# Putting the additions on x in program order between the operand work of h

## The chip, the cores and the metric

One Trainium2 chip, one of its cores. The metric is the device time of one execution in microseconds (us). The kernel before takes 975.35 us, the median of three runs from 972.98 to 976.16.

## The reference, cut to what matters

Attention over keys and values that are averaged in groups of eight, and behind it a gated feed-forward layer, all in fp32:

```python
k_p = k.reshape(B, H, Sp, 8, D).mean(axis=3)        # B = H = 8, S = 576, Sp = 72, D = 64
v_p = v.reshape(B, H, Sp, 8, D).mean(axis=3)
scores = scale * np.matmul(q, k_p.transpose(0, 1, 3, 2))
attn = softmax(scores)
x = np.matmul(attn, v_p)                            # as 4608 tokens x 512
gate = 1.0 / (1.0 + np.exp(-(x @ w_gate)))          # w_gate, w_val: 512 x 1536
return (gate * (x @ w_val) @ w_out)                 # w_out: 1536 x 512
```

## The kernel before, in words

The 4608 tokens are 12 blocks of 384. Blocks 0 and 1 are worked through by a written-out list in a first pass of about 230 us, which also splits the weights into parts and stores them in device memory. The other ten blocks go in five passes, n = 1 to 5, two blocks each. A pass has two stages on TensorE:

- **The gate and value stage** (`hidden`, its matmuls are L621). x of two blocks times the two weight matrices, as two-by-two block products in the seven-product form (Winograd's): products m = 1 to 7 need x11, x12, x21, x22 and sums of them. Every fp32 operand is split into a high and a low part (`fp32r`), so each product term is three matmuls, and one product is six. The results leave PSUM through ScalarE (ACT) copies (L627), VectorE (DVE) additions into a tile `y` (L633), the sigmoid on ACT (L639) and a DVE multiplication (L642), which gives h.
- **The output stage** (`second_sums`, L834). h times w_out in the same seven-product form: 21 units of 12 matmuls, three for each of m = 1, 5, 6, 2, 3, 7, 4. I call them unit 0 to unit 20. The operand of a unit is made by `operand`: DVE sums where needed (`minus`, L766), an ACT cast for the high part (L797) and a DVE subtraction for the low part (L798), into one of four buffers. It is traced two units ahead. After units 11, 14, 17 and 20 the results go out: by DVE (L812), and the last by ACT (L810), into a tile named `o` that shares the two buffers of `y`, and from there by a DMA (L814).

Beside this, the attention of the next two blocks runs, in small steps between the products: scores (L454), exponential (L508, which needs another ACT table than the sigmoid, so an `ACT_TABLE_LOAD` before it and one before the next sigmoid), a transposition of the residual columns (L523) and of the main columns (L542) on TensorE, the product with v (L463) and a copy into `xs` (L553).

x's own operands for the next pass are made by `operands`, a generator of seven steps. Each step is an addition on DVE where one is needed (`combine`, L590), an ACT cast (L167) and a DVE subtraction (L168), the latter two in `split`. The steps come in the order m = 1, 5, 6, 2, 3, 7, 4. One step is drawn after each of units 8, 10, 12, 14, 16, 18 and 20 (`next(build, None)`, L852). The last pass has no next one, so there are four output stages that do this, n = 1 to 4.

What sets the order of instructions on an engine in the five passes: a scheduler, which goes by its own estimate of when each operand is ready and puts an instruction that it thinks ready ahead of others. It may move an instruction far from the place where it was traced. `tc.keep_in_program_order` adds an edge, without a semaphore, from the instruction that was traced just before on the same engine. `in_turn` does that when `tied[0]` is set; L590, L167 and L168 pass through it. Before, the flag is set only for some weight sums of pass 1. All DMAs are issued by SyncE (SP), in its own order, on one queue.

Of the kernel before, what the change touches and what calls it, by code (L numbers as in the profile page):

```python
# [124 lines left out]
def attention_then_ffn(ctx: ExitStack, tc: tile.TileContext, qT, kT, vm, vr, vn, sums8, wgv, wo, const, out, outT):  # L125
# [33 lines left out]
    tied = [False]  # L159
# [198 lines left out]
    def reload_s(m, q):  # L358

        t = opool.tile([P, 2, 2, HALF], F32R, name="oparts")  # L360
        if m < 4:
            half = slice(HALF, DM) if m == 3 else slice(0, HALF)
            for k in range(2):
                f = 4 * q + 2 * k + (m > 1)
                nc.sync.dma_start(t[:, k].bitcast(F32), kept_o[f][:, :, half].bitcast(F32))
        else:
            nc.sync.dma_start(t.rearrange("p k h n -> p k (h n)").bitcast(F32), kept_s[m, q].bitcast(F32))
        oparts[m, q] = t
# [243 lines left out]
    def product(kind, p, m, stays=False):  # L612

        b = {1: "A", 6: "A", 7: "A", 4: "A", 2: "B", 5: "C", 3: "C"}[m]
        if m in (1, 2, 5):
            bank[kind, b] = ps.tile([P, BT], F32, name="chain", tag=CHAIN["GV".index(kind) * 3 + "ABC".index(b)])
        t, w, x = bank[kind, b], parts[kind, p, m] if stays else parts.pop((kind, p, m)), xo[m]
        for c in range(NC // 2):
            a = slice(c * P, (c + 1) * P)
            for k, (h, y) in enumerate(((0, 0), (0, 1), (1, 0))):  # L620
                nc.tensor.matmul(  # L621
                    t, lhsT=w[:, h, a], rhs=x[:, y, c],
                    start=(m in (1, 2, 5) and c == 0 and k == 0), stop=(c == 1 and k == 2), skip_group_check=True,
                )
        if m in (1, 5, 6):
            s = snap.tile([P, BT], F32, name=f"s{kind}{m}")
            nc.scalar.copy(s, t)  # L627
            seen[kind, m] = s
            return
        q = {2: (0, 0), 3: (0, 1), 7: (1, 1), 4: (1, 0)}[m]  # L630
        if m != 4:
            y = two.tile([P, BT], F32, name="y", tag="y")
            nc.vector.tensor_tensor(out=y, in0=t, in1=seen[kind, {2: 1, 3: 6, 7: 5}[m]], op=ALU.add)  # L633
        else:
            y = t
        if kind == "G":
            if m in (2, 7):
                gates[q[0]] = snap.tile([P, 2, BT], F32, name=f"gate{q[0]}")
            nc.scalar.activation(gates[q[0]][:, q[1]], y, AF.Sigmoid)  # L639
        else:  # L640
            f = 2 * p + q[1]
            nc.vector.tensor_tensor(  # L642
                out=hb[f // 4][:, f % 4, q[0] * BT:(q[0] + 1) * BT], in0=y, in1=gates[q[0]][:, q[1]], op=ALU.mult
            )
# [123 lines left out]
    def first_sums(q):  # L768

        at = len(s1)  # L770
        if at == 0:
            s1[None] = big.tile([P, 2, 2, BT], F32, name="s1", tag="big")
            at = 1
        s1[q] = s1[None][:, at - 1] if at < 3 else snap.tile([P, 2, BT], F32, name="s1", tag="gate0")
        minus(s1[q], quarter(q, 1, 0), quarter(q, 1, 1), ALU.add)
        if at < 3:
            third_sums(q)
# [9 lines left out]
    def operand(m, q, n):  # L787

        if m == 6:
            minus(s1[q], s1[q], quarter(q, 0, 0))  # L790
        if m == 3:
            minus(s1[q], quarter(q, 0, 1), s1[q])
        if m == 7 and q == qs[n][2]:
            third_sums(q)
        x = s1[q] if m in (5, 6, 3) else quarter(q, *{1: (0, 0), 2: (0, 1), 7: (1, 0), 4: (1, 1)}[m])
        hs = big.tile([P, 2, 2, BT], F32R, name="hs", tag="big")
        nc.scalar.copy(hs[:, 0], x)  # L797
        nc.vector.tensor_tensor(out=hs[:, 1], in0=x, in1=hs[:, 0].bitcast(F32), op=ALU.subtract)  # L798
        halves[m, q] = hs
# [3 lines left out]
    def second_sums(n, last, build, later):  # L803
        A, B_, C = ("b4", "b5"), ("b0", "b3"), ("b1", "b2")
        acc, seen2 = {}, {}

        def result(side, half, c, bank, add):
            t = two.tile([P, BT], F32, name="o", tag="y")
            if add is None:
                nc.scalar.copy(t, bank)  # L810
            else:
                nc.vector.tensor_tensor(out=t, in0=bank, in1=add, op=ALU.add)  # L812
            r, a = (half * 2 + c) * P, (2 * n - 2 + side) * BT
            nc.sync.dma_start(outT[r:r + P, a:a + BT], t)  # L814

        units = [(m, q) for m in (1, 5, 6, 2, 3, 7, 4) for q in qs[n]]
        for u in units[:2]:
            reload_s(*u)
        for i, (m, q) in enumerate(units):
            if i + 2 < len(units):  # L820
                reload_s(*units[i + 2])
            if i == 1:
                first_sums(qs[n][2])
            if i + 2 < len(units):
                operand(*units[i + 2], n)
            hs = halves.pop((m, q))
            w = oparts.pop((m, q))
            name = {1: "A", 6: "A", 7: "A", 4: "A", 2: "B", 5: "C", 3: "C"}[m]
            for k in range(2):
                for c in range(2):  # L830
                    if i % 3 == 0 and k == 0 and m in (1, 2, 5):
                        acc[name, c] = ps.tile([P, BT], F32, name="acc", tag={"A": A, "B": B_, "C": C}[name][c])
                    for t, (h, y) in enumerate(((0, 0), (0, 1), (1, 0))):
                        nc.tensor.matmul(  # L834
                            acc[name, c], lhsT=w[:, k, h, c * P:(c + 1) * P], rhs=hs[:, y, k],
                            start=(m in (1, 2, 5) and i % 3 == 0 and k == 0 and t == 0), stop=(i % 3 == 2 and k == 1 and t == 2),
                            skip_group_check=True,
                        )
                if i == 0 and k == 1:
                    product("V", TURNS[n][-1], 4, not last)  # L840
            if i % 3 == 2:
                for c in range(2):
                    t = acc[name, c]
                    if m in (1, 5, 6):
                        s = snap.tile([P, BT], F32, name=f"s{'GV'[c]}{m}")
                        nc.scalar.copy(s, t)
                        seen2[m, c] = s
                    else:
                        side, half = {2: (0, 0), 3: (0, 1), 7: (1, 1), 4: (1, 0)}[m]
                        result(side, half, c, t, None if m == 4 else seen2[{2: 1, 3: 6, 7: 5}[m], c])  # L850
            if i >= 8 and i % 2 == 0:
                next(build, None)  # L852
        for _ in build:
            pass
        for _ in range(3):
            next(later, None)
        s1.clear()
# [329 lines left out]
    for n in range(NB // 2):  # L1187
        last = 2 * n + 2 == NB
        tasks, later = ahead[n:n + 2]
        steady[0] = n > 1  # L1190
        if n == 0:
            continue
        if n == 1:
            hidden_second(tasks)
        else:
            hidden(last, tasks, n)
        if last:
            build = iter(())
        else:
            build = operands()  # L1200
        if n < 1:
            second(tasks, build)
        else:
            second_sums(n, last, build, later)
# [46 lines left out]
```

## Time and profile before

| | |
|---|---|
| median of three runs | 975.35 us (972.98, 975.35, 976.16) |
| the profiled execution | 973.47 us, its span 971.7 us |
| granted TensorE clock | 0.993 |
| busy: TensorE matmul, weight loads, DVE, ACT | 97%, 93%, 73%, 57% |
| output stages, by the trace | about 326 to 381, 483 to 536, 632 to 689, 786 to 838 and 922 to 972 us |

Rows are named by engine and line. PE is the matmul side of TensorE and PEld its weight loads, DVE is VectorE, ACT is ScalarE, and SPq is the queue of SyncE that issues the DMAs. A name such as `hs<-s,hs` says what is written and what is read. In the profile's lists of waits the three numbers are the sum in us, how often, and the longest. In its timeline a row begins with the start and the duration in us, and brackets give the idle time of the engine just before and what ended it. Matmuls overlap: one of 384 columns lasts some 0.34 us in a row, but the next one starts 0.175 us after it.

### The profile page before, as it was taken

To read this page: it belongs to the slowest core of one execution; us is meant where nothing else is said; L and a number is where in the kernel's file an instruction comes from. 1 tells how busy PE (TensorE), PEld (TensorE's weight loads), DVE (VectorE), ACT (ScalarE), POOL (GpSimd) and SP (SyncE) were. 2 spreads that over 40 slices of the span, in tenths; PEclk is the share of its full clock that TensorE was granted. 3 is DMA by queue.
4 is the path that set the end of the run, shared out by engine and by line. 5 is a ranking of instruction groups with operands and counts; after the bars stand their busy time and mean duration, and the time that the engine had idled before them with its cause. 6 is when DMAs were issued, how large, how long until landed. Compare 5 with 4: busy or idle time off the path is not lost.

```text
span 971.7 us, 15360 instructions
## 1 busy us (share of the span) xinstructions
PE 939.0 (97%) x5400; PEld 907.2 (93%) x5400; DVE 706.8 (73%) x1231; ACT 557.5 (57%) x1142; POOL 47.5 (5%) x67
## 2 busy tenths in 40 slices
PE   5899999999998999999999999999999999999998
PEld 4689998889998999999999999989999999999998
DVE  7999998787888878767796566599366578244474
ACT  6898966554666656645664555556355555233342
POOL 1210000000000000000000000000000000000000
PEclk8899999999999999999999999999999999999999
DMA  9978987769877377997479878567876637877566
GB/s 317 343 264 311 315 305 219 257 229 352 296 269 245 131 241 247 351 362 247 129 230 277 264 239 275 177 184 255 271 257 221 211 120 227 283 247 251 163 205 228
DMA packets 109883, 243.22 MB, mean 250 GB/s; under 512 B 11376, under 2 KB 45936, under 8 KB 108272
## 3 DMA queue, kind: packets, MB, share of 16 engines
q1 hardware_dynamic: 109808, 242.26, 75.1%
q8 instruction: 43, 0.70, 0.3%
q14 instruction: 32, 0.26, 0.1%
HBM read 191.88 MB, written 50.33 MB: 249 GB/s over the span
## 4 chain that ended last, share of the span: by engine, by line
PE 71%; DVE 15%; DMA 7%; ACT 4%; issue 2%; SPq 0%; DVEq 0%; ACTq 0%
PE chain L621 38%; PE acc L834 18%; PE chain L661 5%; PE acc L1147 3%; PE sc L454 3%; PE av L463 2%; DVE s L766 2%; DVE hs L798 1%; DMA out<-o 1%; DMA raw<-in_wgv 1%; DVE raw L197 1%; DVE w L199 1%; PE tp L542 1%; DVE zs L975 1%; DMA parts<-keptG1A 1%
## 5 line engine op out<-in xcount | busy, mean ns | idle before, releaser
L621 PE MATMUL chain<-xo,parts 128*128 128x384 f32 x2436 | 457.5, 341 | 7.6 <-ACT sG L627 2.5
L621 PEld LDWEIGHTS chain<-xo,parts 128*128 128x128 f32 x2436 | 424.0, 188 | 12.1 <-ACT sG L627 3.7
L834 PE MATMUL acc<-hs,oparts 128*128 128x384 f32 x1260 | 229.2, 336 | 3.2 <-DVE hs L798 2.8
L834 PEld LDWEIGHTS acc<-hs,oparts 128*128 128x128 f32 x1260 | 218.2, 188 | 6.0 <-DVE hs L798 4.4
L633 DVE TENSOR_TENSOR y<-chain,sG 128x384 f32<-128x384 f32 x87 | 47.8, 552 | 79.1 <-ACT sG L627 27.6
L661 PE MATMUL chain<-xo,parts 128*128 128x384 f32 x504 | 93.7, 340 | 0.8 <-ACT xs L1086 0.8
L661 PEld LDWEIGHTS chain<-xo,parts 128*128 128x128 f32 x504 | 87.9, 188 | 2.6 <-ACT xs L1086 1.1
L627 ACT COPY sG<-chain 128x384 f32<-128x384 f32 x87 | 41.5, 477 | 55.5 <-PE chain L621 55.1
L633 DVE TENSOR_TENSOR y<-chain,sV 128x384 f32<-128x384 f32 x87 | 47.5, 550 | 35.1 <-PE chain L621 26.4
L798 DVE TENSOR_TENSOR hs<-h,hs 128x768 fp32r<-128x768 f32 x60 | 58.1, 973 | 17.1 <-ACT hs L797 17.1
L627 ACT COPY sV<-chain 128x384 f32<-128x384 f32 x87 | 41.3, 476 | 50.0 <-PE chain L621 45.5
L639 ACT ACTIVATE gate<-y 128x384 f32<-128x384 f32 x87 | 45.5, 525 | 41.2 <-DVE y L633 40.7
L797 ACT CAST hs<-h 128x768 fp32r<-128x768 f32 x60 | 49.9, 834 | 25.4 <-PE acc L834 25.1
L536 POOL TENSOR_TENSOR pm<-e,rz 128x384 f32<-128x384 f32 x32 | 29.2, 912 | 610.7 <-DVE rz L516 224.7
L797 ACT CAST hs<-s 128x768 fp32r<-128x768 f32 x45 | 37.0, 835 | 34.4 <-PE acc L834 22.7
L1147 PE MATMUL acc<-oparts,hs 128*128 128x512 f32 x216 | 51.7, 392 | 0.4 <-DVE hs L1137 0.4
L642 DVE TENSOR_TENSOR h<-y,gate 128x384 f32<-128x384 f32 x87 | 49.0, 567 | 1.8
L798 DVE TENSOR_TENSOR hs<-s,hs 128x768 fp32r<-128x768 f32 x45 | 42.5, 954 | 8.3 <-ACT hs L797 8.0
L1147 PEld LDWEIGHTS acc<-oparts,hs 128*128 128x128 f32 x216 | 40.2, 188 | 8.7 <-DVE hs L1137 0.8
L454 PE MATMUL sc<-kbd,raw 128*128 128x144 f32 (+1 forms) x280 | 47.6, 308 | 0.0
L454 PEld LDWEIGHTS sc<-kbd,raw 128*128 128x128 f32 (+1 forms) x280 | 38.3, 187 | 6.6 <-issue 4.0
L546 DVE TENSOR_TENSOR pl<-tp,ph 128x384 fp32r<-128x384 f32 x32 | 17.6, 551 | 26.7 <-ACT ph L545 26.7
(186 smaller groups left out, 1182.0 us busy)
## 6 DMA issues: line engine op xcount, KB each, us to landing
oparts<-keptS SPq DMA_DIRECT2D x60, 512.0 KB, 4.4
oparts<-keptO SPq DMA_DIRECT2D x90, 256.0 KB, 3.8
raw<-in_wgv SPq DMA_DIRECT2D x12, 1024.0 KB, 6.7
raw<-in_qT SPq DMA_DIRECT2D x42, 192.0 KB, 4.3
out<-o SPq DMA_DIRECT2D x40, 192.0 KB, 4.3
raw<-in_kT SPq DMA_DIRECT2D x26, 288.0 KB, 4.1
raw<-in_vm SPq DMA_DIRECT2D x28, 256.0 KB, 4.1
raw_o<-in_wo SPq DMA_DIRECT2D x12, 512.0 KB, 4.4
```

The costliest lines, as they stand in the source:

```text
L454: nc.tensor.matmul(sc[lo - i * P:hi - i * P, i], lhsT=q[:, lo:hi], rhs=kbd[slot(b, p)], start=True, stop=True)
L536: nc.gpsimd.tensor_tensor(out=pm, in0=e[:, n, :, :KM], in1=rz[:, n, :, None].broadcast_to([P, 2 * QT, KM]), op=ALU.mult)
L621: nc.tensor.matmul(t, lhsT=w[:, h, a], rhs=x[:, y, c], start=(m in (1, 2, 5) and c == 0 and k == 0), stop=(c == 1 and k == 2), skip_group_ ...
L627: nc.scalar.copy(s, t)
L633: nc.vector.tensor_tensor(out=y, in0=t, in1=seen[kind, {2: 1, 3: 6, 7: 5}[m]], op=ALU.add)
L639: nc.scalar.activation(gates[q[0]][:, q[1]], y, AF.Sigmoid)
L642: nc.vector.tensor_tensor(out=hb[f // 4][:, f % 4, q[0] * BT:(q[0] + 1) * BT], in0=y, in1=gates[q[0]][:, q[1]], op=ALU.mult)
L661: nc.tensor.matmul(t, lhsT=w[:, c // 2, h, a], rhs=x[:, y, c % 2], start=(c == 0 and k == 0), stop=(c == NC - 1 and k == 2),)
L797: nc.scalar.copy(hs[:, 0], x)
L798: nc.vector.tensor_tensor(out=hs[:, 1], in0=x, in1=hs[:, 0].bitcast(F32), op=ALU.subtract)
L834: nc.tensor.matmul(acc[name, c], lhsT=w[:, k, h, c * P:(c + 1) * P], rhs=hs[:, y, k], start=(m in (1, 2, 5) and i % 3 == 0 and k == 0 and ...
L1147: nc.tensor.matmul(acc[i], lhsT=hss[f][:, y, a], rhs=oparts[f][:, w], start=(f == 0 and k == 0), stop=(f == NF - 1 and k == 2),)
```

## The change

The flag is set around the draw of a step of x's operands in the output stage, so that each of the step's instructions gets an edge from the instruction traced just before on its engine. Nothing is computed otherwise, and no instruction is added or removed.

```diff
                         side, half = {2: (0, 0), 3: (0, 1), 7: (1, 1), 4: (1, 0)}[m]
                         result(side, half, c, t, None if m == 4 else seen2[{2: 1, 3: 6, 7: 5}[m], c])
             if i >= 8 and i % 2 == 0:
+                tied[0] = True
                 next(build, None)
+                tied[0] = False
         for _ in build:
             pass
```

```python
    def in_turn(instruction):
        if tied[0]:
            tc.keep_in_program_order(instruction)
    def split(h, l, x):
        in_turn(nc.scalar.copy(h, x))
        in_turn(nc.vector.tensor_tensor(out=l, in0=x, in1=h.bitcast(F32), op=ALU.subtract))
```

The edges change what the scheduler sees as next, so that from the first output stage on it orders all engines but GpSimd anew. Three places follow.

The first is DVE in the output stage of pass 3, from unit 5's low part to unit 8's. An `L798` row makes the low part of one unit's operand. `xo_...` and `s<-s,xs` are x's, `s_6549` and `s_7201` with `h` are h's, `m`, `e`, `ks` and `vs` are attention's. Before:

```order
L500 TENSOR_REDUCE m<-sc 128x6
L798 TENSOR_TENSOR hs<-s_7201,hs 128x768
L798 TENSOR_TENSOR hs<-s_6549,hs 128x768
L503 TENSOR_TENSOR e<-sc,m 128x432
L397 TENSOR_REDUCE ks<-raw 128x72
L798 TENSOR_TENSOR hs<-s_6549,hs 128x768
L168 TENSOR_TENSOR xo_7400<-s,xo_7400 128x768
L766 TENSOR_TENSOR s_7201<-s_7201,h 128x768
L766 TENSOR_TENSOR s_6549<-h,s_6549 128x768 x2
L590 TENSOR_TENSOR s<-s,xs_6050 128x768
L500 TENSOR_REDUCE m<-sc 128x6
L798 TENSOR_TENSOR hs<-s_7201,hs 128x768
```

The same place now, with the rows up to x's first one:

```order
L798 TENSOR_TENSOR hs<-s_7201,hs 128x768
L798 TENSOR_TENSOR hs<-s_6549,hs 128x768
L418 TENSOR_TENSOR vl_103<-vs,vh_98 64x64 x2
L766 TENSOR_TENSOR s_7201<-s_7201,h 128x768
L798 TENSOR_TENSOR hs<-s_6549,hs 128x768
L766 TENSOR_TENSOR s_6549<-h,s_6549 128x768 x2
L798 TENSOR_TENSOR hs<-s_7201,hs 128x768
L798 TENSOR_TENSOR hs<-h,hs 128x768
L766 TENSOR_TENSOR s_7201<-h,s_7201 128x768
L798 TENSOR_TENSOR hs<-h,hs 128x768
L168 TENSOR_TENSOR xo_7357<-xs_6050,xo_7357 128x768
```

x's subtraction (L168) and addition (L590) and attention's maximum (L500) left the stretch between unit 7's low part and unit 8's. Between unit 4's low part and unit 5's, ahead of it, one L168, one L590 and one L500 left as well, one L766 moved ahead of unit 4's, an L397 stands for another L397, and an L546 came. x's rows now stand one by one between the L798 rows of units 10 to 20, and the last two behind unit 20's. The output stages of passes 2 and 4 have the same picture; before, their x rows stood from unit 2 on, the first two even in the gate and value stage.

The second place is TensorE at the end of the output stage of pass 3 and the products behind it. `acc` rows are the output stage's (here the end of unit 20), `chain` rows the next pass's products, six matmuls each. Before:

```order
L834 MATMUL acc_7182<-hs_7558,oparts_7556 128x384 x3
L542 MATMUL tp_7684<-cst_87,pm_7682 128x128 x3
L621 MATMUL chain_7702<-xo3_7530,parts_6963 128x384 x6
L621 MATMUL chain_7652<-xo7_7574,parts_6963 128x384 x6
L621 MATMUL chain_7830<-xo6_7448,parts_7015 128x384 x3
L621 MATMUL chain_7943<-xo2_7491,parts_7015 128x384 x6
L621 MATMUL chain_7844<-xo5_7400,parts_6983 128x384 x6
L463 MATMUL av_7713<-ph_7688,vh4_100 128x192
```

Seven more `L463` rows of 192 columns follow there, then six matmuls of `chain_7830<-xo7_7574`, then `chain_8047`, the first product that needs a bank which a `y` addition must have read. Now:

```order
L834 MATMUL acc_7182<-hs_7558,oparts_7556 128x384 x3
L621 MATMUL chain_7702<-xo3_7530,parts_6963 128x384 x6
L621 MATMUL chain_7652<-xo7_7574,parts_6963 128x384 x6
L621 MATMUL chain_7830<-xo6_7448,parts_7015 128x384 x6
L621 MATMUL chain_7943<-xo2_7491,parts_7015 128x384 x5
L621 MATMUL chain_7844<-xo5_7400,parts_6983 128x384 x6
L621 MATMUL chain_7943<-xo2_7491,parts_7015 128x384
L621 MATMUL chain_7830<-xo7_7574,parts_7035 128x384 x6
L454 MATMUL sc_7620<-kbd3_94,raw_7612 64x144
L454 MATMUL sc_7620<-kbd3_94,raw_7612 128x144
L621 MATMUL chain_8047<-xo2_7491,parts_7763 128x384 x6
```

Three more matmuls of products stand there now (36 for 33), and the attention's eight L463 and three L542 left; two L454 came.

The third place is ACT around the end of the output stage of pass 2. Before, attention's first exponential stands within the output stage, with the table load ahead of it, between casts of h:

```order
L797 CAST hs<-s_4904 128x768
L167 CAST xo_5813<-s 128x768
L797 CAST hs<-s_4904 128x768
L508 ACT_TABLE_LOAD
L508 ACTIVATE e<-e 128x864
L797 CAST hs<-s_5566 128x768
L797 CAST hs<-h 128x768 x2
```

Now it stands behind the stage's last results (L810), between sigmoids of the next pass (L639):

```order
L810 COPY o<-acc 128x384 x2
L167 CAST xo_5972<-xs_4757 128x768
L627 COPY sV_6198<-chain 128x384
L639 ACTIVATE gate_6079<-y 128x384 x2
L627 COPY sV_6151<-chain 128x384
L639 ACTIVATE gate_6117<-y 128x384
L508 ACT_TABLE_LOAD
L508 ACTIVATE e<-e 128x864
L639 ACT_TABLE_LOAD
L639 ACTIVATE gate_6117<-chain 128x384
```

The number of table loads is the same, and in passes 3 and 4 all four exponentials of a pass now stand in the gate and value stage, where there were three. The last cast of x (`xo_5972`) stands behind the L810 rows. The attention's last products with v now reach into the first units of the output stages 3 and 4.

## The prediction

> **What bounds the kernel now.** I read the page's busy shares first, then PEld's list of waits from 225 us on (the part that the change reorders lies behind it), then the windows of the stages.
>
> ```profile
> PE 939.0 (97%) x5400; PEld 907.2 (93%) x5400; DVE 706.8 (73%) x1231; ACT 557.5 (57%) x1142; POOL 47.5 (5%) x67
> ...
> PEld acc L834 <- DVE hs L798: 4.4, 5, 1.3
> PEld chain L621 <- ACT sG L627: 3.7, 4, 2.1
> PEld chain L621 <- DVE y L633: 2.4, 2, 1.3
> PEld chain L621 <- ACT gate L639: 0.8, 1, 0.8
> PEld chain L621 <- DMA parts<-keptG1A: 0.7, 1, 0.7
> ```
>
> TensorE is the bound: any time that can be won is a hole in its rows. I count on PEld, because a matmul's row runs on while its successor waits: the same five waits for `hs` read 2.8 us on PE and 4.4 us on PEld, and it is the later start of the next weight load that the end of the kernel feels. The list says what there is: 4.4 us for h's low parts (L798), 2.4 us for `y` behind the output stages, 4.5 us for ACT's copies and gates. Of the whole span of 971.7 us that is little.
>
> ```profile
> core 0: us, PE busy (x) PEld busy (x) DVE busy (x) ACT busy (x) POOL busy (x), PEclk, DMA share, GB/s
> 483.00:536.00 53.00, 52.79 (x313) 52.26 (x312) 41.00 (x59) 27.32 (x42) 1.33 (x1) 1.00 0.78 242
> 632.00:689.00 57.00, 55.14 (x317) 53.31 (x317) 43.97 (x62) 28.53 (x47) 1.33 (x1) 1.00 0.72 234
> 786.00:838.00 52.00, 51.26 (x293) 50.43 (x292) 37.68 (x48) 24.26 (x35) 0.00 (x0) 1.00 0.72 231
> ...
> 632.00:655.00 23.00, 22.04 (x126) 20.61 (x125) 20.88 (x29) 11.80 (x20) 0.00 (x0) 1.00 0.60 182
> 679.00:689.00 10.00, 10.00 (x61) 9.95 (x60) 0.97 (x3) 1.48 (x4) 0.00 (x0) 1.00 0.88 305
> ```
>
> The first three rows are the output stages of passes 2, 3 and 4. DVE looks no more than 77% busy in the middle one, but the last two rows cut that stage: 20.9 of 23 us at its start, 1.0 of 10 us at its end. So DVE is the limit of the first units and idle in the last ones. The waits for L798, window by window (the three output stages in order):
>
> ```profile
> PEld acc L834 <- DVE hs L798: 0.5, 1, 0.5
> ...
> PEld acc L834 <- DVE hs L798: 2.5, 2, 1.3
> ...
> PEld acc L834 <- DVE hs L798: 1.4, 2, 0.7
> ```
>
> They add up to the 4.4 us. In the timeline of pass 3 one sees TensorE stop twice, and what DVE did before:
>
> ```profile
> 647.26 4.11 PE L834 MATMUL acc<-hs,oparts 128*128 128x384 f32 x22 [0.87 <-DVE hs L798]
> 655.90 5.84 PE L834 MATMUL acc<-hs,oparts 128*128 128x384 f32 x32 [1.00 <-DVE hs L798]
> ...
> 649.17 0.95 DVE L798 TENSOR_TENSOR hs<-s,hs 128x768 fp32r<-128x768 f32 x1
> 650.04 0.95 DVE L168 TENSOR_TENSOR xo<-s,xo 128x768 fp32r<-128x768 f32 x1
> 650.91 0.95 DVE L766 TENSOR_TENSOR s<-s,h 128x768 f32<-128x768 f32 x1
> 651.77 1.82 DVE L766 TENSOR_TENSOR s<-h,s 128x768 f32<-128x768 f32 x2
> 653.51 0.95 DVE L590 TENSOR_TENSOR s<-s,xs 128x768 f32<-128x768 f32 x1
> 654.38 0.60 DVE L500 TENSOR_REDUCE m<-sc 128x6 f32<-128x432 f32 x1
> 654.90 0.95 DVE L798 TENSOR_TENSOR hs<-s,hs 128x768 fp32r<-128x768 f32 x1
> ...
> 487.23 0.55 DVE L546 TENSOR_TENSOR pl<-tp,ph 128x384 fp32r<-128x384 f32 x1
> 487.70 0.68 DVE L397 TENSOR_REDUCE vs<-raw 128x64 f32<-128x512 f32 x1
> 490.50 0.46 DVE L418 TENSOR_TENSOR vl<-vs,vh 64x64 fp32r<-64x64 f32 x2
> ```
>
> The last three rows, from another place, are for two later terms. Behind a 768-wide DVE row the next one starts after 0.87 us, behind an L546 after 0.47; an L397 lasts 0.7 us. Between the low parts of units 7 and 8 stand 5.7 us of DVE work, of which an L168, an L590 and an L500 (0.87 + 0.87 + 0.52 = 2.3 us) are not h's.
>
> **What the change removes.** By the order now, x's rows stand at units 10 to 20 and behind. In pass 3, between unit 4's and unit 8's low parts, two L168, two L590, two L500, an L503 and one L397 go (4 x 0.87 + 3 x 0.52 + 0.7 = 5.7 us), one L766 moves ahead, and an L546 (0.47) and two L418 (0.4) come. That is some 4.8 us less, the moved L766 not counted, against the 2.5 us of waits: they go whole. In pass 4 two L168 and two L590 go there, 3.5 us, and an L546 comes in ahead of unit 5; so 3.0 us less against 1.4 us. In pass 2 x's three rows and more leave, against 0.5 us. I take all of it: **-4.4 us**. Bounds: the 2.8 us that PE's rows show, and 4.4 us.
>
> Where x's rows went: behind unit 10, h needs only L798 and now and then a result, so a unit's DVE work is 0.9 to 2.7 us and on average 1.75, with one x row of 0.87 in most units, against 12 matmuls x 0.174 = 2.1 us on TensorE. The cover is there, by 0.35 us a unit, and nineteen matmuls of the next products (3.3 us) stand on TensorE between units 17 and 18. If it went, each of the eleven x rows would cost up to 0.87 us. On ACT, 7 casts spread over a stage that is busy 28.5 of 57 us are hidden too. Tied in order, each x row is a wait for what is ahead: behind the L168 of `xo_7400` in the order stand a result (L812) and unit 14's low part. What they all wait for is unit 11's end, two units ahead of their use. Zero. x's last cast is now behind the L810 rows, at the very end of the stage. Its product, m = 4 on the gate side, comes after 36 product matmuls, 6.3 us, and the cast and subtraction take 0.8 + 1.0 us. Zero.
>
> **What it adds.** First, the end of a stage. The result tiles share `y`'s two buffers, so the first `y` addition waits until L814's DMA has landed:
>
> ```profile
> 688.96 1.00 ACT L810 COPY o<-acc 128x384 f32<-128x384 f32 x2 [6.83 <-DMA oparts<-keptO]
> 689.89 0.86 SPq L814 DMA_DIRECT2D out<-o  x2
> 696.62 1.02 DVE L633 TENSOR_TENSOR y<-chain,sG 128x384 f32<-128x384 f32 x2 [4.29 <-DMA out<-o]
> 697.23 0.82 PEld L621 LDWEIGHTS chain<-xo,parts 128*128 128x128 f32 x5 [1.08 <-DVE y L633]
> ...
> 536.20 5.00 PE L621 MATMUL chain<-xo,parts 128*128 128x384 f32 x27
> 541.75 3.50 PE L621 MATMUL chain<-xo,parts 128*128 128x384 f32 x19
> ...
> 542.39 1.12 DVE L633 TENSOR_TENSOR y<-chain,sG 128x384 f32<-128x384 f32 x2 [4.78 <-DMA out<-o]
> ...
> 846.01 2.05 PEld L621 LDWEIGHTS chain<-xo,parts 128*128 128x128 f32 x12 [1.33 <-DVE y L633]
> ```
>
> Until then TensorE lives on what needs no `y`. Behind pass 3 that was 33 matmuls and attention's L463 and L542, from the stage's end at about 689.3 to 697.23 - 1.08 = 696.15, 6.9 us, and then it waited 1.1 us; now it is 36 x 0.175 and two short L454, some 0.3, 6.6 us: +0.3. Behind pass 2 `y` was read at 542.39 + 0.56 = 542.95, and TensorE came there at 541.75 + 6 x 0.175 = 542.8, 6.9 us behind the stage's end; now, with 36 matmuls and three L454, after 6.6 us: +0.3. Behind pass 4 the 36 matmuls stay: 0. So **+0.6 us**. Bounds: 0, and four ends with 1.3 us each less the 2.4 that are there, +2.8. This is what is late next: DVE's relief ends at a DMA that starts only with the stage's last result.
>
> Second, two exponentials with their pairs of table loads move into the gate and value stages of passes 3 and 4. What one does there:
>
> ```profile
> 570.65 1.28 ACT L508 ACT_TABLE_LOAD   x1
> 571.94 0.93 ACT L508 ACTIVATE e<-e 128x864 f32<-128x864 f32 x1
> 572.89 1.28 ACT L639 ACT_TABLE_LOAD   x1
> ...
> 576.24 1.32 PE L621 MATMUL chain<-xo,parts 128*128 128x384 f32 x6 [0.66 <-ACT sG L627]
> ...
> PEld chain L621 <- ACT sG L627: 1.0, 1, 1.0
> ```
>
> ACT is held 3.5 us, and the copies that free TensorE's banks queue behind it. In pass 3's stage (536 to 632) three such events cost 1.8 us on PEld (the 1.0 here and the gate's 0.8 of the first list), in pass 4's three cost nothing: 0.3 us an event, so **+0.6 us** for two. Bounds: 0, and 2.1 us each (the longest wait for sG in the first list), +4.2.
>
> The Trainium skill prices this higher: ScalarE: Activation LUTs, under "What ACT_TABLE_LOAD costs", gives a switch of tables 1.28 us and another 1.38 us of drain. With that the two events would hold ACT 5.5 us longer, and the time would come to 975.8 us at worst instead of 970.3. The rows disagree: the exponential starts at 571.94, right where the load ends, so this way gets a chance of 0.02.
>
> Everything else (the same instructions, reordered within their stages) I take at nothing, covered by TensorE's queue; the waits of 0.7 us and less for weights may fall otherwise.
>
> **The sum.** -4.4 + 0.6 + 0.6 = -3.2 us, made against the profiled execution: 973.47 - 3.2 = 970.3 us (span 968.5). That execution lay 1.9 us under the median of the three, so the median goes to **972.2 us**.
>
> **The rivals.** A, the relief is only half: another DVE row takes the place (the L546 ahead of unit 5 waits for attention's transposition, and h's low parts stand behind it). Then -2.2 + 1.2 = -1.0: 974.4. For it, that this row stands there in both passes; against it, POOL and TensorE did that work in time before.
>
> B, the time comes back as waits for data. The DMA engines are 0.72 to 0.78 busy in these stages, 0.88 at the end of pass 3's. A stage that ends 2.5 us earlier asks for its weights earlier, and `y` waits for a DMA. Then about 0: 975.4. Against it, the waits for `parts` are 0.7 us at most.
>
> C, slower: the gate and value stages of passes 3 and 4 get all four exponentials each, and ACT's copies become the limit there. Eight events at the mean of the three that were felt (2.1, 1.0, 0.8: 1.3 us) cost 10.4 in place of 1.8: +8.6 - 4.4 + 0.6 = +4.8, that is 980.2. It turns slower than before from 0.7 us an event. For it, pass 3's stage; against it, pass 4's, where three events went unfelt.
>
> D, the edges hold nothing back, or the scheduler undoes them: the order speaks against it, no chance of its own.
>
> E, more: the reordered ends need no wait for `y` at all, -4.4 - 2.4 + 0.6 = -6.2: 969.2. It takes a DMA that lands 1.3 us earlier, and nothing starts it earlier.
>
> **How the numbers follow.** Forecast 0.60, A 0.10, B 0.09, C 0.12, E 0.07, and 0.02 for the longer switches that the page states. A measurement of this kernel cannot tell less than 0.3%, 2.9 us, from no change. The forecast has its centre just beyond that, with bounds from -5.5 (no costs, and the 1.1 us behind pass 3 gone too) to -1.6 us (2.8 won, costs as taken); I give two thirds of it, 0.40, to faster, the rest to no change. With E: faster 0.47. No change: 0.20 + A + B + 0.02 = 0.41. Slower: C, 0.12. The likeliest one's own range is 969.9 to 973.8; for 8 in 10, with E, A, B and the near side of C, 968.7 to 977.2.
>
> **What would show it.** Right: no wait of TensorE for L798 in the three output stages; DVE's x rows between units 10 and 20; the first wait behind the stages still for `y`, some tenths longer. Wrong: waits for L798 that stay (A), longer waits for `parts` or `y` (B), waits for sG, sV or gate in passes 3 and 4 above 0.7 us for each exponential (C). If the waits for L798 are gone and the time is not, the place where TensorE stands instead is the answer.

## The result, and the profile after

The changed kernel takes 978.88 us (median of 8 runs, 977.32 to 981.65), the kernel before in the same session 973.75 us (8 runs, 972.98 to 976.23). The ratio is 1.0052, with a 95% interval of 1.0038 to 1.0066: some 5.1 us slower, where 3.2 us less were forecast. The profiled execution has a span of 977.0 us, against 971.7 before. (Line numbers of the changed kernel are higher by 2 behind L852.)

Here are the page's busy times of the changed kernel, and PEld's waits from 225 us on down to 1.4 us (engine, waiting line, what it waited for; us in total, times, longest).

```profile
PE 940.7 (96%) x5400; PEld 907.8 (93%) x5400; DVE 709.8 (73%) x1231; ACT 558.1 (57%) x1142; POOL 47.7 (5%) x67
...
PEld sc L454 <- issue: 4.3, 20, 0.3
PEld chain L621 <- DVE y L633: 3.8, 3, 2.2
PEld chain L621 <- ACT sG L627: 3.6, 4, 2.1
PEld chain L621 <- ACT gate L639: 2.5, 1, 2.5
PEld acc L834 <- issue: 1.9, 3, 1.1
PEld chain L621 <- ACT parts L167: 1.8, 1, 1.8
PEld chain L621 <- ACT sV L627: 1.6, 1, 1.6
PEld chain L621 <- issue: 1.4, 7, 0.2
```

The 4.4 us of waits for h's low parts (L798) are gone to the last one; no row of the whole list names L798. In their place stand a wait of 2.5 us for a gate, 1.6 us for sV, and 3.8 us for `y` in place of 2.4. Sorted by stage, as the sum over all weight loads that start more than 200 ns behind the one ahead, of what lies beyond the usual 174 ns (worked out from PEld's rows, in us):

| stage | before | after |
|---|---|---|
| gate and value stage of pass 2 | 3.3 | 5.5 |
| output stage of pass 2 | 0.6 | 0.1 |
| gate and value stage of pass 3 | 2.2 | 5.2 |
| output stage of pass 3 | 3.6 | 0.1 |
| gate and value stage of pass 4 | 2.2 | 4.3 |
| output stage of pass 4 | 1.6 | 0.0 |
| gate and value stage of pass 5 | 2.0 | 3.8 |
| output stage of pass 5 | 1.2 | 2.1 |

The output stages of passes 2 to 4 win 5.6 us, the gate and value stages lose 9.1, and the last output stage 1.0. The largest loss is in pass 3's stage, and most of it stands in one place, some 12 us behind the stage's start. This is the changed kernel's timeline of ACT and PE there:

```profile
546.54 1.28 ACT L508 ACT_TABLE_LOAD   x1 [1.63 <-DVE e L503]
547.83 0.92 ACT L508 ACTIVATE e<-e 128x864 f32<-128x864 f32 x1
548.77 1.28 ACT L639 ACT_TABLE_LOAD   x1
550.07 0.49 ACT L639 ACTIVATE gate<-chain 128x384 f32<-128x384 f32 x1
...
550.61 1.68 PE L621 MATMUL chain<-xo,parts 128*128 128x384 f32 x8 [2.26 <-ACT gate L639]
```

One of attention's exponentials, which stood in pass 2's output stage before, holds ACT from 546.5 to 550.1, and the gate that frees TensorE's bank stands behind it. The place in the stage is not what makes it dear. The kernel before also has an exponential there, and TensorE did not wait. There the same gate, the fourth of the stage, stood ahead of it:

```profile
547.39 0.49 ACT L639 ACTIVATE gate<-chain 128x384 f32<-128x384 f32 x1 [0.23 <-PE chain L621]
548.54 1.28 ACT L508 ACT_TABLE_LOAD   x1 [0.65 <-DVE e L503]
549.83 0.93 ACT L508 ACTIVATE e<-e 128x864 f32<-128x864 f32 x1
```

The exponential at 547.8 came here because its maxima (L500) did. At the end of pass 2's output stage in the changed kernel, the first of them stands right behind the subtraction of x's last product, which waits 8.4 us for its cast:

```profile
536.86 0.96 DVE L168 TENSOR_TENSOR xo<-xs,xo 128x768 fp32r<-128x768 f32 x1 [8.35 <-ACT xo L167]
537.73 0.60 DVE L500 TENSOR_REDUCE m<-sc 128x6 f32<-128x432 f32 x1
```

Pass 3's output stage is the same. These are the L500 rows alone in its window, before and (second fence) after (window, length, busy us and number of rows, clock, DMA share, GB/s):

```profile
632.00:689.00 57.00, 1.21 (x2) 1.00 0.72 234
```

```profile
635.00:688.00 53.00, 0.00 (x0) 1.00 0.70 234
```

VectorE's order of the changed kernel at the end of that stage has the same reason. The kernel pins attention's reductions (L397, L500) from pass 2 on behind what is traced ahead of them on VectorE, and that is the subtraction of x's last product (`xo4`). Before, the subtraction and the first L397 behind it stood early in pass 3's stage (641.5 and 642.4 us), between units 4 and 5. With its edge, `xo4` is the last of the stage, and L397 stands behind it:

```
L168 TENSOR_TENSOR xo4_7607<-xs1_6422,xo4_7607 128x768
L397 TENSOR_REDUCE ks_7614<-raw_7615 128x72
L633 TENSOR_TENSOR y_7759<-chain_7752,sG1_7659 128x384
```

Another loss stands behind the output stage of pass 4. Here is the changed kernel's timeline of SP's queue, ACT, DVE and PE, and then PE's windows there:

```profile
838.01 2.49 SPq L365 DMA_DIRECT2D oparts<-keptO  x4
841.56 1.08 SPq L814 DMA_DIRECT2D out<-o  x2
...
840.62 1.00 ACT L810 COPY o<-acc 128x384 f32<-128x384 f32 x2 [5.25 <-PE acc L834]
...
848.69 1.71 DVE L633 TENSOR_TENSOR y<-chain,sG 128x384 f32<-128x384 f32 x3 [5.35 <-DMA out<-o]
...
849.31 3.92 PE L621 MATMUL chain<-xo,parts 128*128 128x384 f32 x12 [1.86 <-DVE y L633]
```

```profile
846.00:849.40 3.40, 1.54 (x10) 1.00 1.01 384
849.68:852.88 3.20, 3.20 (x11) 0.50 0.16 62
```

And the kernel before, SP's queue and DVE at the same place:

```profile
834.54 3.25 SPq L365 DMA_DIRECT2D oparts<-keptO  x4
839.12 0.86 SPq L814 DMA_DIRECT2D out<-o  x2
...
845.40 1.71 DVE L633 TENSOR_TENSOR y<-chain,sG 128x384 f32<-128x384 f32 x3 [15.64 <-DMA out<-o]
```

Four weight loads for the next output stage (L365) are issued 3.55 us before the results' DMA where it was 4.58 us before, as SP waits for TensorE's last units to free their buffers. From the DMA's issue to `y` it takes 7.1 us, and it took 6.3 us (848.69 - 841.56, 845.40 - 839.12). That the loads ahead in the queue are what delays it is read from the order of issue and not proved by itself; behind the last output stage, where no loads are left in the queue, the results land 1.8 us after their issue in both kernels. TensorE waited 2.2 us there (1.3 before), and then ran for 3.2 us at half its clock, 11 matmuls where 3.2 us hold 18, which costs another 1.5 us (ten starts 146 ns late).

### The profile page after: what moved, and what is told of

Same layout as the page of the kernel before. It is cut to its first block, busy times and chain, and to the rows that moved or that the text cites. A ratio compares the mean times of both kernels' runs of the same rounds, so it can differ in the third digit from the quotient of the medians.

```text
span 977.0 us, 15351 instructions
## 1 busy us (share of the span) xinstructions
PE 940.7 (96%) x5400; PEld 907.8 (93%) x5400; DVE 709.8 (73%) x1231; ACT 558.1 (57%) x1142; POOL 47.7 (5%) x67
## 4 chain that ended last, share of the span: by engine, by line
PE 73%; DVE 13%; DMA 7%; ACT 4%; issue 2%; SPq 1%; DVEq 0%; ACTq 0%
PE chain L621 36%; PE acc L834 22%; PE chain L661 5%; PE acc L1149 3%; PE sc L454 3%; PE av L463 2%; DVE w L199 1%; DVE raw L197 1%; PE tp L542 1%; DMA keptG5C<-sums 1%; DMA raw<-in_kT 1%; DMA out<-o 1%; DMA oparts<-keptS 1%; DVE zs L977 1%; DMA w<-keptwV 1%
## 5 line engine op out<-in xcount | busy, mean ns | idle before, releaser
L639 ACT ACTIVATE gate<-y 128x384 f32<-128x384 f32 x87 | 45.6, 525 | 42.6 <-DVE y L633 42.0
L797 ACT CAST hs<-h 128x768 fp32r<-128x768 f32 x60 | 50.1, 835 | 31.9 <-PE acc L834 31.5
L798 DVE TENSOR_TENSOR hs<-h,hs 128x768 fp32r<-128x768 f32 x60 | 58.0, 973 | 11.3 <-ACT hs L797 11.0
L797 ACT CAST hs<-s 128x768 fp32r<-128x768 f32 x45 | 37.3, 837 | 29.6 <-PE acc L834 22.6
L454 PE MATMUL sc<-kbd,raw 128*128 128x144 f32 (+1 forms) x280 | 49.7, 311 | 0.6 <-ACT early L973 0.6
L798 DVE TENSOR_TENSOR hs<-s,hs 128x768 fp32r<-128x768 f32 x45 | 42.5, 953 | 8.7 <-ACT hs L797 8.3
L454 PEld LDWEIGHTS sc<-kbd,raw 128*128 128x128 f32 (+1 forms) x280 | 38.9, 187 | 8.3 <-issue 5.6
L168 DVE TENSOR_TENSOR xo<-xs,xo 128x768 fp32r<-128x768 f32 x12 | 11.5, 955 | 32.0 <-ACT xo L167 32.0
```

The lines of the kernel that those rows point to most:

```text
L454: nc.tensor.matmul(sc[lo - i * P:hi - i * P, i], lhsT=q[:, lo:hi], rhs=kbd[slot(b, p)], start=True, stop=True)
```

## The experiments

The theories. **M**: VectorE's relief is real; the loss comes with attention's rows, which the edge on x's last product also holds back. **S**: the loss is ScalarE's table switches, now at the heads of the gate and value stages. **L**: the loss is `y` waiting for the results' DMA. **V**: the relief itself is worth nothing, since the next wait takes its place. **R**: any new order made by the scheduler costs 3 to 5 us. Each kernel was timed in five rounds beside the kernel before.

### The relief alone

In x_rows_alone the order of every engine is written out in a table and enforced by edges of order (no waits):

```
+ for each engine: for (earlier, later) in its table:
+     tc.add_manual_dep(later, earlier, NoSync)
```

The table is the order before, in which the rows of six of x's products have moved on VectorE and ScalarE, in three output stages.

> Every engine's order is written out as it stood before, TensorE's, SP's and GpSimd's to the last row; on VectorE and ScalarE alone, in the output stages of passes 2, 3 and 4, x's rows for products 1, 5, 6, 2, 3 and 7 stand where the change has them (x's product 4 stays where it was). This is what the prediction priced, without anything that the scheduler did besides. Theory M (the relief is real, the loss comes with attention's rows, which the edges also hold back): the waits of TensorE for L798 fall from 4.4 us to under 1 us and the time falls by 3 to 4.5 us, 969 to 971 us. Theory V (VectorE's relief only hands the waits on to ScalarE, the weights or y): 973 to 975 us, no change.

Measured 971.78 us beside 974.93, ratio 0.9968 (0.9952 to 0.9984): 3.1 us faster, as M says; V, which gave no change, is out. Among its PEld waits from 380 us on are:

```profile
PEld chain L621 <- DVE y L633: 1.6, 2, 1.1
PEld acc L834 <- ACT hs L797: 1.3, 2, 1.2
PEld acc L834 <- DVE hs L798: 1.2, 1, 1.2
PEld chain L621 <- ACT sG L627: 1.2, 2, 1.0
```

Of the 4.4 us for L798, 1.2 remain (M: under 1 us), and one wait of 1.2 us has come at ScalarE's cast of h. Both stand in pass 3's output stage and have a cause in the timeline:

```profile
646.37 0.61 DVE L500 TENSOR_REDUCE m<-sc 128x6 f32<-128x432 f32 x1 [0.72 <-PE sc L454]
646.89 1.82 DVE L798 TENSOR_TENSOR hs<-s,hs 128x768 fp32r<-128x768 f32 x2
...
658.56 0.96 DVE L168 TENSOR_TENSOR xo<-xs,xo 128x768 fp32r<-128x768 f32 x1 [1.79 <-ACT xo L167]
659.43 0.60 DVE L503 TENSOR_TENSOR e<-sc,m 128x432 f32<-128x432 f32 x1
```

An L500 waits for TensorE's scores with two of h's low parts behind it, and x's first product waits 1.8 us for its cast with attention's L503 behind it, so that the exponential and the cast behind that come late. In x_rows_tuned L500 stands behind the two low parts, and x's first product behind the exponential.

> The order of x_rows_alone with two places mended in pass 3's output stage: attention's first L500, which held the low parts of units 5 and 6 until TensorE's scores (1.2 us), stands behind them, and x's product 1 stands behind the exponential that came late through it (1.2 us at an L797). Theory M: both waits go, 2 us less than x_rows_alone: 969.5 to 970.5 us beside 975. Theory V: the time stays at that of x_rows_alone (972).

Measured 970.91 us beside 974.01, ratio 0.9960 (0.9945 to 0.9975). Both waits of 1.2 us are gone. PEld's list from 380 us on still has 0.4 us for L797, as before the change, and 0.2 us for L798; some of its rows:

```profile
PEld chain L621 <- DVE y L633: 2.0, 2, 1.4
PEld chain L621 <- ACT sG L627: 1.1, 2, 0.9
PEld chain L621 <- ACT gate L639: 0.8, 1, 0.8
PEld acc L834 <- ACT hs L797: 0.4, 2, 0.2
```

The waits went as M says; the time fell by only 0.8 us beyond x_rows_alone where M had 2, and the intervals do not separate the two. This kernel beats both the one before and the change.

### Which edges

```
- tied[0] = True
+ tied[0] = i < 20      (x4_free: all but x's last product)
+ tied[0] = i == 20     (x4_alone: only x's last product)
```

> The changed kernel with the edges on six of the seven steps, not on the last (x's product 4, step after unit 20). Attention's next rows (L397, L500) stand in the program behind that step's subtraction and are pinned behind it; with the edge off, they come back into the output stages of passes 2 and 3. Theory M: the waits in the gate and value stages of passes 3 and 4 fall back to about those before (5.2 and 4.3 us to 2.2 each), the waits for L798 stay under 2 us: 970 to 973 us. Theory R (any new order that the scheduler makes costs some 3 to 5 us, wherever attention stands): 976 to 980 us.

> The kernel before with the edge on the last step alone (x's product 4). Attention's rows are held out of the output stages as in the change, the other six products' rows are free. Theory M: the loss without the relief's full size: the gate and value stages of passes 3 and 4 wait 4 to 5 us each as in the change, 977 to 981 us. Theory V or the opposite of M (the loss comes from the other six steps): as before, 973 to 975 us. Theory R: 976 to 980 us as well.

x4_free: 975.08 us beside 974.93, ratio 0.9999 (0.9985 to 1.0013). x4_alone: 977.66 us, 1.0029 (1.0012 to 1.0046). In x4_free two L500 are back in pass 3's output stage, and PEld's waits in the stage behind it (536.5 to 633.9) are:

```profile
PEld chain L621 <- DVE y L633: 1.0, 2, 0.7
PEld chain L621 <- ACT sG L627: 1.0, 1, 1.0
PEld chain L621 <- ACT ph L545: 0.9, 1, 0.9
```

The gate's 2.5 us are gone. In x4_alone no L500 stands in that output stage, and the exponential is in the next stage again, with the gate behind it (ACT's load and PE):

```profile
547.54 1.28 ACT L508 ACT_TABLE_LOAD   x1 [2.01 <-DVE e L503]
...
550.17 1.32 PE L621 MATMUL chain<-xo,parts 128*128 128x384 f32 x6 [1.16 <-ACT sG L627]
551.98 1.32 PE L621 MATMUL chain<-xo,parts 128*128 128x384 f32 x6 [0.48 <-ACT gate L639]
```

So the last product's edge costs some 5 us on top of the other six (1.0052 against 0.9999), and 2.8 us by itself. The 2.8 us are what is left when the relief is paid for: x4_alone has no wait for L798 either. Its time lies in the ranges of M and of R and does not tell them apart. x4_free lies between M's range and R's: it is 3.0 us behind x_rows_alone, which has the same 1.2 us left for L798, and the two differ mainly in what the scheduler did with the other rows. That part is R.

> The changed kernel with attention's three steps at the end of an output stage not pinned behind what is traced ahead of them; x's seven steps keep their edges. If the pin alone held attention back (theory M), its first rows return to the output stages and the time falls to 971 to 974 us; in the order, though, only pass 2's output stage gets some of them back, so that M expects 975 to 978 us there. Theory R: 976 to 980 us.

```
+ steady[0] = False     (around the three steps of attention at the stage's end)
```

977.80 us, ratio 1.0033 (1.0019 to 1.0046): in the ranges of both. The profile tells more. With the pin off, attention's rows do go back, and further than they stood before. Counted in order, the exponential that the change has at 547.8 stands in pass 2's output stage (485 to 540 here), and the one that the change has at 706.0 stands ahead of pass 3's (640 to 694):

```profile
489.30 0.93 ACT L508 ACTIVATE e<-e 128x864 f32<-128x864 f32 x1
...
632.37 0.93 ACT L508 ACTIVATE e<-e 128x864 f32<-128x864 f32 x1
```

No wait for L798 is left, and yet the gate and value stages of passes 2 to 5, summed as in the table, wait 16.3 us (9.7 before, 18.8 in the change). So the pin does decide where attention's rows stand, but to have them early again is worth only 1.9 us here, and the intervals leave it between nothing and 3.7. This is against M as the whole cause.

### Table switches

```
- nc.scalar.activation(gates[q[0]][:, q[1]], y, AF.Sigmoid)
+ nc.scalar.activation(gates[q[0]][:, q[1]], y, AF.Tanh)
```

The same in the other two places where gates are made. With tanh the 35 table loads go (ACT has 1107 rows in place of 1142), so none is needed between it and the exponential here; no other row changes its place.

> The kernel before with the gates' sigmoid replaced by tanh (the numbers of the gates are changed by this). The 35 table loads of ScalarE go, the order on TensorE, VectorE and ScalarE stays the same otherwise. Theory S (the loss of the change is ScalarE's table switches, which now stand at the heads of the gate and value stages): TensorE's waits that stand behind a switch here are 0.4, 2.1, 1.0 and 0.8 us, so some 4 us less, plus what the first 225 us give. Theory L (the loss is VectorE's y additions that wait for the results' DMA): the same here, it says nothing of this kernel alone.

> The changed kernel with the gates' sigmoid replaced by tanh (the numbers of the gates are changed by this); the same order, without the 35 table loads. Theory S: the waits behind a switch were 0.4, 2.1, 1.6, 2.5, 0.5, 0.8 and 0.3 us in the changed kernel, 8.2 us against 4.3 us before; without them the changed kernel stands only some 1.2 us above the kernel before that is built in the same way (5.1 - 3.9), and not more than 2.5 us. Theory L: the waits for y stay (3.8 us against 2.4) with the slow 3 us behind the longest, and the distance stays at 4 us or more.

before_tanh: 972.17 us beside 974.71, ratio 0.9974 (0.9960 to 0.9987). after_tanh: 975.56 us, 1.0011 (0.9996 to 1.0026). The switches cost 2.5 us before (some 4 were expected) and 4.0 us in the changed kernel. The distance falls from 5.1 to 3.6 us; S expected 2.5 at most and L at least 4, so S is not the whole. Its part of 1.5 us is not clear of noise: the three intervals, added as squares, leave it between -0.9 and 3.9 us. In after_tanh the exponential stands at the same place in pass 3's stage, and TensorE runs through behind it:

```profile
548.65 0.93 ACT L508 ACTIVATE e<-e 128x864 f32<-128x864 f32 x1 [1.65 <-DVE e L503]
...
550.17 6.04 PE L621 MATMUL chain<-xo,parts 128*128 128x384 f32 x32
```

So at that place the loads make the wait of 2.5 us. But the same profile has another wait in its place: 2.6 us for a weight (`keptV2B`) in pass 2's stage, where the changed kernel waited 0.2.

### The results' buffers

First the last two results of a stage were given the free buffers of `seen` copies, and the scheduler was left to order the rows:

```
- t = two.tile([P, BT], F32, name="o", tag="y")
+ t = (snap.tile([P, BT], F32, name="o", tag=("sV1", "sV6")[c]) if add is None
+      else two.tile([P, BT], F32, name="o", tag="y"))
```

> The changed kernel with the last two results of an output stage (m = 4) in buffers that nothing else needs at that time, so that y no longer waits for their DMA. The scheduler may put other rows otherwise. Theory L: the three waits for y (0.8, 0.9, 2.2 us) and the half pace behind the last (1.5 us) go: 5.3 us less, 973.6 us. Theory S: the waits for y go, but ScalarE's copies behind the exponentials hold TensorE at nearly the same places: 1 to 2 us less, 977 to 978 us.

> The kernel before with the same two buffers. Both theories: its two waits for y (1.1 and 1.3 us) go, 2.4 us less, 971.3 us; if the distance to the changed kernel with these buffers is then under 2 us, L holds, if it is over 4 us, S.

after_own_o 976.76 us beside 974.71, ratio 1.0028 (1.0015 to 1.0042); before_own_o 979.62 us, 1.0060 (1.0040 to 1.0081). Neither theory has the second: one thing less to wait for, and 5.8 us slower. The order on TensorE, VectorE and ScalarE changed with it, and the loss is in waits of 0.4 to 1.3 us all over the kernel. This is R, and it says that a kernel which the scheduler orders anew cannot price one wait. So the next two have the order written out as it stood, and differ in the buffers alone:

```
- t = two.tile([P, BT], F32, name="o", tag="y")
+ t = (big if add is None else two).tile([P, BT], F32, name="o", tag="big" if add is None else "y")
```

> The changed kernel with every engine's order written out as the change has it, and one thing different: the last two results of an output stage (m = 4) go to buffers of hs's kind, which are free then, so that y needs no result's DMA. Theory L (the part of the loss that is not attention's exponentials is the late landing of the results): the waits for y (3.8 us, with 1.5 us at half pace behind the longest) go: 974 to 975.5 us beside 979 to 980. Rival: y's additions then wait for the copies of ScalarE that stand beside them, 1 us less at most: 978 to 979.

> The kernel before, order written out as it stood, with the same two buffers. Its waits for y are 1.1 and 1.3 us: theory L gives 2.4 us less, 972.5 beside 975 us; the rival at most 1 us less.

after_o_apart 975.00 us beside 974.01, ratio 1.0010 (0.9990 to 1.0029); before_o_apart 973.45 us, 0.9989 (0.9977 to 1.0001). The change wins 4.1 us by it, as L says, and the kernel before 1.1 us, nearer to the rival's 1 us than to L's 2.4: L is worth 3.0 us of the difference, between 0.4 and 5.6 by the intervals. No run has the order written out and nothing else changed; that before_o_apart is no slower than the kernel before says that writing it out costs no time that can be told.

> x_rows_tuned with the results' buffers apart. Theory L: its waits for y (0.5 and 1.1 us) go as well: 968 to 969 us. Rival: 969.5 to 970.5, no change against x_rows_tuned.

970.10 us beside 974.01, ratio 0.9959 (0.9942 to 0.9976): no change that can be told from x_rows_tuned, as the rival says. Its waits for `y` are gone, and 1.8 us for L797 stand in the last output stage of the profiled execution.

### Both, and where the rest is

> The changed kernel's order with both taken away: tanh in place of the gates' sigmoid (no table loads; the gates' numbers are changed by this), and the last two results in buffers apart. Additive (table switches 4.0 us, results' buffers 4.1 us): 8 us less than the changed kernel, 971 to 972 us beside 975 before. If each only uncovers waits that the other leaves: 974 to 975 us.

> The kernel before with both taken away in the same way (the gates' numbers are changed by this). Additive (2.5 and 1.1 us): 3.6 us less, 971 to 972 us. With after_both additive as well, the two kernels end within 1 us of each other, and the relief of 3.1 us is still paid for by some 3 to 4 us of other waits in the changed kernel.

after_both 970.44 us beside 974.27, ratio 0.9965 (0.9950 to 0.9979); before_both 970.45 us, 0.9955 (0.9942 to 0.9969). Nearly additive: the distance is 1.0 us where it was 5.1, no more than noise. But the relief of 3.1 us is in after_both as well, so that some 4 us of other waits are still in it. Summed as in the table of stages, the output stages of passes 2 to 5 wait 1.6 us in it and 8.2 in before_both, and the gate and value stages 11.7 and 4.9. Its list of waits has more for the weights:

```profile
PEld sc L454 <- issue: 4.0, 19, 0.3
...
PEld chain L621 <- DMA parts<-keptG3B: 2.7, 3, 1.1
PEld chain L621 <- DMA parts<-keptV2B: 1.6, 1, 1.6
```

In before_both these rows read 3.5 us for L454 and 1.2 us for keptG3B, and keptV2B has none. The weights come late, and attention's scores, of which none is left in the output stages of passes 2 and 3 (28 matmuls stood there before), interrupt the products more often: 24 times in place of 19 from 326 us on. How the 6.9 us divide between the two was not measured.

The last two kernels put the orders together at the first matmul of pass 2's output stage, where both orders have done the same work but for at most six rows of an engine.

> Order written out: on every engine the order of the changed kernel up to the first matmul of pass 2's output stage, and from there that of the kernel before. Theory P (the part of the loss that neither the results' buffers nor the table switches explain stands in pass 2's gate and value stage, which begins between 1.9 us later with sigmoid and 4.5 us later with tanh): 1.9 to 4 us slower than before, 977 to 979 us beside 975. Rival: pass 2 loses nothing by itself, 974 to 976.

> The other half: the order before up to the first matmul of pass 2's output stage, and from there that of the changed kernel, with the relief of VectorE in the output stages of passes 2, 3 and 4. Theory P: by the profiles the rest of the change costs 2.7 us, 977 to 978 us beside 975. Rival: all of the loss is here, 979 to 980.

changed_to_pass2 976.87 us beside 974.27, ratio 1.0026 (1.0011 to 1.0041); changed_from_pass2 978.24 us, 1.0045 (1.0026 to 1.0064). P holds for the first half, 2.5 us: no relief is in this half to speak of, only a new order. In its timeline a weight (0.8 us at 406.1) and a copy of ScalarE (1.0 us at 410.2) hold TensorE. The second half costs 4.4 us rather than 2.7, as much as the rival says; its interval (2.5 to 6.2 us) does not decide between the two. Its profiled execution has the gate's wait again (2.5 us, ended at 551.8) and half a clock behind it. The halves add up to 6.9, not 5.1; the intervals allow either.

## Why the prediction was wrong

The step that failed is the last of the sum: "Everything else (the same instructions, reordered within their stages) I take at nothing, covered by TensorE's queue". x_rows_alone moves x's rows as priced, for six of the seven products, keeps the rest in its old order, and is 3.1 us faster; the change, with all that the scheduler reordered beside them, is 5.1 us slower. So what came beside the relief costs 8.2 us (6.1 to 10.3, the two intervals added as squares), where the prediction had 0.6 + 0.6 = 1.2. It is paid in the gate and value stages, also in pass 2's and pass 5's, for which the prediction took nothing. The terms one by one:

- **What bounds the kernel**: right. By the table TensorE's holes make 4.5 us of the 5.3 us between the two spans, and PEld's rows showed them.
- **What the change removes, -4.4**: right in mechanism, near in size. The waits for L798 go whole in the changed kernel, and the move of x's rows alone is worth 3.1 us (1.6 to 4.7 by its interval). "4.8 us less" on VectorE against 2.5 us of waits was too kind for x's rows alone: one of pass 3's two waits belonged to attention's L500.
- **The end of a stage, +0.6**: this step failed in size. "Behind pass 4 the 36 matmuls stay: 0" counted what TensorE has to do and took the landing of the DMA as it was. The landing came 0.8 us later, the wait grew by 0.9 us, and the longer hole was followed by 1.5 us at half pace in the profiled execution. By the change's list the waits for `y` are 0.8, 0.8 and 2.2 us behind passes 2, 3 and 4, against 0, 1.1 and 1.3; with the half pace that is 2.9 us more. The runs with the buffers apart give 3.0 (0.4 to 5.6).
- **The exponentials, "0.3 us an event"**: failed in size too. The mean over six events, of which four went unfelt, was taken for one that has the gate of a waiting bank right behind it: 2.5 us there. The bound of 2.1 us each was too low as well. Of the 2.5 us the table loads are the cause, as after_tanh's profile shows; how much of the 5.1 us the loads make in all (1.5 us by the medians) the runs do not settle.
- **"Everything else"**: not covered. The new order up to pass 2's output stage, which holds next to no relief, costs 2.5 us (1.1 to 4.0), and some 4 us in all are left, among them late weights and more interruptions by attention's scores, when the two terms above are taken away. These parts overlap and do not add up to the 8.2.
- **The moved rows**: the prediction priced the two exponentials as side effects. It did not see why they moved: L397 and L500 are pinned behind x's last subtraction, and with the pin off they stand early again. "x's last cast is now behind the L810 rows ... Zero" looked at the product that needs it, and not at what stands behind its subtraction on VectorE, which waits 8.4 us for that cast. Without the edge on that subtraction the change is some 5 us faster, without the pin only 1.9.
- **The rivals**: C had the right place and direction (waits for sG and gate above 0.7 us in pass 3), but wanted eight events of 1.3 us; there was one of 2.5 and none of the others above 0.8, and the rest came from B's kind of waits, for `y` and the weights. No rival had both at once, and C's 0.12 was too little.
- **What would show it**: this part served. The waits for L798 were gone and the time was not, and TensorE stood in the gate and value stages instead.

What stays open: why to take off the pin wins so much less than to take off the edge, though attention's rows stand early in both; whether the L365 loads ahead in the queue are what makes the results land later; and the split of the last 4 us between the weights and attention's scores, which no run took apart.

## What to carry to other kernels

An edge of order drags along whatever is pinned behind the instruction it holds: look for what is traced next on that engine before tying the last of a group. When a scheduler orders a program anew, a term of 4 us that was read off the profile can be right and still be lost among small waits elsewhere; to price it, write the old order out and move only the rows in question. Price a moved exponential by the rows that stand right behind it on its engine, not by the mean over places where others could run ahead.

## What the runs showed of the hardware

A hole of some 2 us on TensorE can halve its clock for the next 3.2 to 3.4 us. The rows behind pass 4 have it at 849.68 (granted 0.50); the same hole of 2.5 us in pass 3's stage had it in changed_from_pass2 and not in the changed kernel. PE's windows of changed_from_pass2:

```profile
549.10:551.80 2.70, 0.41 (x4) 1.00 0.89 334
552.60:555.80 3.20, 3.20 (x12) 0.50 0.44 134
```

and of the changed kernel:

```profile
547.90:550.60 2.70, 0.45 (x4) 1.00 0.87 308
551.40:554.70 3.30, 3.30 (x21) 1.00 0.52 185
```

In the 18 profiles there are 30 holes of 1.9 us or more in PEld's rows behind 225 us, and 14 of them were followed by 9 to 11 matmuls at a pace of 320 ns in place of 174, some 1.5 us each time; no other slow stretch stands there. The Trainium skill (TensorE: Matmul & The Clock Gate, under "What's actually happening") gives half rate after at least one idle window of 3.4 us, in windows that run freely. The length of the slow stretch agrees; that a hole shorter than a window is enough, about every second time, is what the runs add.
